# Weight rows laid out as one run per partition, strided columns, a halved last tile and a new order

## Chip, cores and metric

The kernel runs on one core of one Trainium2 chip. The metric is device time of one execution in microseconds: 153.68 us as the median of three runs (153.36 to 154.52). The engines are TensorE (PE, with its weight loads shown apart as PEld), VectorE (DVE), ScalarE (ACT), GpSimd (POOL) and SyncE (SP, which here only issues transfers).

## The reference

Two stages. A gated linear attention runs over 768 steps for 4 x 8 heads of size 48; its output, 3072 tokens of 384, goes through a feed-forward layer whose hidden value is the maximum of three products.

```python
for t in range(S):
    state = alpha[:, :, t, :, None] * state + einsum('bhd,bhe->bhde', k[:, :, t], v[:, :, t])
    y[:, :, t] = einsum('bhd,bhde->bhe', q[:, :, t], state)
x = y.transpose(0, 2, 1, 3).reshape(3072, 384)
h = maximum(maximum(x @ w1, x @ w2), x @ w3)      # w1, w2, w3: 384 x 768
out = h @ w_out                                   # w_out: 768 x 384
```

## The kernel before

The tokens are cut into 12 units (3 stretches of 256 steps for each of 4 batches), each unit into two halves of 4 heads ("pairs" below are numbered 0 to 23) and, for the feed-forward layer, into two tiles of 128 tokens, m = 0 to 23. Each unit needs four loads of 384 KB (alpha, q, k, v; `load`, L262), issued from SP; unit 0 is loaded in halves. The weights are transferred from POOL (`weights`, L272) and turned from f32 to f16 on the way.

The attention of a unit runs through these steps, each with its own engine: the product of the two alphas of a step pair (`aa`, L324, POOL or DVE), its logarithms (L329 and L334, ACT), head totals (L344, PE) and their exponentials (L351), sums of logarithms over the steps (L389, PE; L393, DVE), exponentials of both signs (L398, ACT), scaled q and k (L403, POOL or DVE), their transposes (L421, PE; copied by L429, DVE), scores (L441, PE), masked scores (L449, DVE), the state's sums and carries (L472, L486, L492, L373), and the output y as a sum of two products (L509, L531, PE). Then `xb` copies y from PSUM as f16 times a factor (L247 on ACT, L249 on DVE), L551 transposes it on PE, and L243 copies the transposed tile to `xT`.

The feed-forward layer uses max(a, b, c) = a + max(0, b - a, c - a). `differences` (L281, six instructions on DVE) forms w2 - w1 and w3 - w1 in `wcat`, in place. `bypass` forms w1 @ w_out once: three groups of transposes of `w1s` (L294, PE) and three products (L307), kept in `past`. For each unit, `ffn` has six groups of six matmuls (L575; j = 0 to 2 picks 256 hidden columns, g the difference), with a relu for g = 0 (L584 on ACT, L586 on DVE) and a maximum for g = 1 (L591, DVE), and per tile m one output accumulation of three matmuls with `past` (L603) and six with `wo16` (L606), its copy to `ob` (L243) and its transfer out (L618, SP). The last unit's output accumulations are emitted in two parts, so that the first part needs only two of the three pieces of hT.

No scheduler decides at run time. Every step is registered in a plan; the string `ORDER` lists step numbers with an engine letter and the PSUM banks, and `emit` walks through it. Each engine executes its own instructions in that order and waits where its next instruction isn't ready, so what stands behind a waiting instruction waits too. PSUM has 8 banks, named in `ORDER` as well.

The layouts that the change touches: partition p of `w1s`, `wcat` and `wo16` holds rows p, 128 + p, 256 + p and so on, so one weight row is one contiguous piece of the transfer, and feature tile t of `xT` holds features 128 t to 128 t + 127.

Of the kernel before, what the change touches and what calls it, by code (L numbers as in the profile page):

```python
# [26 lines left out]
6S 0S 3S 1S 2S 52S 5S 7S 8V 9A 4S 10A 11G 17P0 54S 18V 13A 53S 19A 14P1 98S 28P2 12A 20A 55S 29V  # L27
15A 22V 100S 30A 31A 21V 99S 56V 101S 24P3 16G 143S 58A 32V 145S 57A 33V 74P5 144S 59P6 25V 62P7
35P0 146S 23A 63V 205S 26P2 64A 36V 272S 65A 34A 206S 75V 37P0 67G 27V 207S 60A 40P47 77A 274S 76A
61G 339S 66V 208S 42V 78G 69P2 38V 273S 39G 79V 41V 73G 81P5 68A 102G 82V 70V 83P0 80G 104A 44P4  # L30
85G 84V 86P56 45P2 87V 71P0 88V 46A 119P3 72V 103A 47P5 90P2 49A 120V 91P4 122A 193P0 92V 95A 105P1
121A 89V 108P4 93P2 48A 43V 96P3 50P6 123V 51A 94A 124V 109V 126P5 111A 97A 195P7 189V 106A 187V
196A 262P2 127V 321P3 194A 188V 128P5 110A 113V 254P1 112G 129V 258P7 255A 130G 329P0 115P4 192V
330A 197P1 107G 116V 114A 125G 331P6 198A 190V 117P4 325P0 322A 118V 147G 148A 256P1 191V 149A
131P34 263A 257V 153P5 259A 264P2 154V 133V 326A 132V 164P1 260P7 156A 265V 327P0 165V 261V 167A
135P3 323P2 166A 332V 155A 136P7 324V 169G 201P1 140V 158G 150P6 199P5 202A 137A 157V 151A 168V
160P2 328V 171P6 203P1 159A 170G 172V 200A 161V 173P6 204A 175P05 209G 174V 162P2 333P1 211A 163V
276G 277A 210A 218P6 269P7 334A 152G 219V 539S 278A 176V 275S 134V 221A 340S 177V 220A 141P2 229P3
138P1 341S 285P4 222G 230V 179P0 139A 266P6 142V 406S 231A 286V 342S 232A 223V 288A 234G 279P1
180P2 270A 267V 287A 212P3 178V 392P7 181A 233V 213A 296P6 225P4 280A 215G 184A 297V 236P2 290G  # L40
394P1 226V 299A 298A 237V 301G 182P0 393A 388P4 183V 344A 185P5 343G 238P2 395V 224A 227P6 336P0
186A 228V 289G 235A 389A 214G 239V 217G 390P1 337A 216G 345A 292P5 338S 300G 240P74 473S 293V 363P0
352P2 396P3 408S 353V 241V 474S 354A 463P5 391V 397A 268S 242G 398P6 335S 291A 282G 243V 409S 461P7
464A 281G 364V 302G 407S 399V 366A 459P3 284G 271S 365A 244V 476S 245P1 355A 246P5 460V 307P60 671S
357G 247P 462V 605S 294P2 251A 465P4 283G 295V 248A 356G 252P7 411A 455P5 253A 308V 368G 457P1 456A
466V 249P2 359P6 410G 458V 250A 303P3 346P5 529P2 304V 310G 412A 525P1 360V 309G 347A 530A 367G
305P3 311V 369A 361P5 521P7 306V 526A 349G 350G 358A 312P2 523P0 351G 522A 362V 543G 313P1 413P3
419P4 430P7 314P 414A 431V 370P5 420V 433A 467P3 524V 315A 435G 371V 318A 421A 477G 372P0 422A
374P25 545A 470P6 436G 479A 375V 478A 348G 373V 376G 432A 379P4 434G 480P2 471A 403P7 468A 424V
377V 486P0 319P1 423G 404A 531P6 487V 378V 488A 405S 380P3 527P7 481A 532V 608S 320A 541S 489A 381P  # L50
609G 528V 544A 475S 426P1 437P5 382A 540S 415G 316P0 427V 503G 400P7 317A 438V 416G 385V 383P4
552P1 401V 386P2 384A 591P0 483V 387A 402S 553V 484G 428P5 672S 592A 439P3 675G 497P7 555A 655P2
440V 554A 425G 593P0 611A 485G 498V 589P1 500A 418V 429V 491G 546P3 499A 653P4 587P7 417G 654A 594V
441P56 547A 676A 490V 563P4 533P3 442V 588V 443G 444G 656V 661P0 534A 501G 564V 447P5 535S 663P7
590V 662A 606S 492G 677A 446P2 445V 657P3 674S 565A 502G 664V 542S 566A 493P0 448P 658V 472S 482G
556G 504P6 607S 494V 508P4 624A 469S 659P3 452A 449V 610A 618P0 505V 595P1 450P5 453P2 596V 597P6
451A 454A 509V 536P7 660V 511G 549G 619V 568G 598V 621A 506P1 495P4 620A 678P3 551G 537A 725P6 496V
569G 679A 538S 684P0 612P7 719P3 557G 673S 685V 507V 665P4 567G 550V 686A 629P5 695P1 548V 599P2
510V 613A 720A 681V 623V 666A 615V 683V 723P7 622G 696V 630V 698A 602P3 724V 631A 614G 558G 687A
726V 635A 688G 721P4 697A 600V 603A 512P7 700G 601S 513P0 722V 632A 625P1 667S 514P 604S 626V 699G  # L60
574P6 515A 559P3 570P1 518A 727P5 634G 571V 701A 519P7 575V 729P0 616G 728A 560V 577G 516P1 668P2
633G 517V 730V 520V 627P5 669A 572P3 689V 561P0 737P7 670S 617V 573V 731P2 738A 562V 741P7 732A
578P3 576V 745P4 742A 628V 690A 579P0 636P1 580P 637V 640P7 581A 691P5 584V 638P1 746A 582P3 692V
747P0 583A 641V 644P4 743P5 639V 642G 739P6 643G 680V 585P3 645P7 740V 702P1 586A 646P 682V 706P3
703V 647A 734P6 650A 748V 707V 744V 704P1 709G 693P3 759P7 708G 735V 694V 755P0 757P5 705V 711P6
752P3 710P4 761P1 753A 756A 754S 648P2 712P 760A 733S 651P3 649A 749P0 762V 652A 716V 713V 777P7
750A 763P2 751S 736S 717P1 714P3 781P6 718A 779P4 782V 765P0 715V 783P1 778V 799P6 764V 801P3 766V
800A 773P7 784V 775P2 758V 793P0 780V 797P6 774V 795P1 791P5 767P4 792V 802V 770P7 776V 768A 796V
769S 794V 785P5 798V 771V 803P3 786V 772S 787S 807P4 804P 808P 805V 788P2 809A 806S 810S 789A 790S
# [44 lines left out]
def kernel(  # L114
# [82 lines left out]
    xTs = homes(NG, [P, NFT, TG], FP16, "xT")  # L197
# [70 lines left out]
    def weights(g):  # L268
        w, dst = ((moe_w1, moe_w2, moe_w3, moe_w_out)[g],
                  (w1s, wcat[:, :, 0, :], wcat[:, :, 1, :], wo16)[g])  # L270
        plan.step("weights", "POOL", -1.0,
                  lambda eng: nc.gpsimd.dma_start(dst, w.rearrange("(t p) f -> p t f", p=P)),  # L272
                  writes=[("w", g)], size=1.25 if g == 3 else 1.0)


    def differences():
        for g in range(2):
            for j in range(NJ // 2):
                cols = slice(2 * j * P, (2 * j + 2) * P)
                plan.step("d", "DVE", LEAD - 0.5 + 0.5 * g,  # L280
                          lambda eng, g=g, cols=cols: nc.vector.tensor_sub(  # L281
                              wcat[:, :, g, cols], wcat[:, :, g, cols], w1s[:, :, cols]),
                          reads=[("w", 0), ("w", g + 1)], writes=[("d", g, j)])


    def bypass():
        rank = LEAD + 0.5 * SLOPE
        for kt in range(NFT):
            wk = ("wt", kt)

            def turn(eng, kt=kt, wk=wk):
                live[wk] = bank(wk, [P, NJ, P], FP16)
                for j in range(NJ):
                    nc.tensor.transpose(live[wk][:, j, :], w1s[:, kt, j * P:(j + 1) * P], ident)  # L294
# [201 lines left out]
    def output(n):  # L496
# [43 lines left out]
        for i in range(UB):  # L540
# [4 lines left out]
                          eng, xb, live[yk].rearrange("p a b -> p (a b)"), ysc),  # L545
                      reads=[yk], writes=[("xb", m % 3)])

            def turn(eng, xb=xb, xk=xk):
                live[xk] = bank(xk, [P, NFT, P], FP32)
                for ft in range(NFT):  # L550
# [6 lines left out]
                      reads=[xk], writes=[("xT", n, i)])  # L557


    def ffn(n):  # L560
# [32 lines left out]
        for i in range(UB):  # L593
            m = n * UB + i
            r = rank[2 * (NJ // 2) + i]
            ok = ("op", m)
            parts = [(0, NJ)] if n < NG - 1 else [(0, NJ - 2), (NJ - 2, NJ)]
            for lo, hi in parts:
                def shrink(eng, i=i, ok=ok, lo=lo, hi=hi):
                    if lo == 0:  # L600
                        live[ok] = bank(ok, [P, DM], FP32)
                        for kt in range(NFT):
                            nc.tensor.matmul(live[ok], xT[:, kt, i * P:(i + 1) * P],  # L603
                                             past[:, kt, :], start=(kt == 0), stop=False)
                    for kt in range(lo, hi):
                        nc.tensor.matmul(live[ok], hT[:, kt, i * P:(i + 1) * P], wo16[:, kt, :],  # L606
                                         start=False, stop=(kt == NJ - 1))

                plan.step("op", "PE", r + (0.5 if lo else 0.0), shrink,
                          size=hi - lo + (NFT if lo == 0 else 0),  # L610
                          banks=[ok] if lo == 0 else [], writes=[ok],
                          reads=[("hT", n % 3, j) for j in range(lo // 2, hi // 2)]
                          + [("w", 3)]
                          + ([("xT", n, i)] + [("past", kt) for kt in range(NFT)]) * (lo == 0))
            plan.step("ob", "ACT DVE", r, lambda eng, m=m, ok=ok: copy(eng, obs[m % 4], live[ok]),
                      reads=[ok], writes=[("ob", m % 4)])
            plan.step("out", "SP", -2.0,
                      lambda eng, i=i, m=m: nc.sync.dma_start(  # L618
                          out[b * S + (2 * c + i) * P:b * S + (2 * c + i + 1) * P, :], obs[m % 4]),
                      reads=[("ob", m % 4)])  # L620

    load(0, 0, HH, "aqk")
    load(0, HH, H, "a")
    load(0, 0, HH, "v")
    load(0, HH, H, "qkv")
# [49 lines left out]
```

## Time and profile before

| | |
|---|---|
| median of three runs | 153.68 us |
| the profiled execution | 153.0 us |
| its span (first to last instruction) | 151.2 us |
| granted clock | 0.998 |
| PE / DVE / ACT / POOL busy | 133.5 / 120.7 / 82.3 / 69.3 us |
| first matmul of the feed-forward layer (L575) | 28.14 us |
| last matmul ends | 147.85 us |
| issue of w1, w2, w3, w_out on POOL | 15.81, 16.76, 19.09, 30.89 us |

Times inside the execution count from the span's start. An idle engine matters only where the end waits for it. The profile puts a wait down to whatever came last. The chain of work that ended last is followed backwards from the last instruction, and tells which engine or transfer the end hung on at each moment.

### The profile page before, as it was taken

What the parts mean: (1) busy time and instruction counts of PE and PEld (TensorE: products, weight loads), DVE (VectorE), ACT (ScalarE), POOL (GpSimd) and SP (SyncE); (2) the same over time, 40 slices, a digit from 0 to 9 for tenths busy, and PEclk for the clock granted to TensorE, in tenths of its full rate; (3) what the DMA queues carried; (4) which work ended last, traced back from release to release, by engine and by line L of the source; (5) the groups of instructions that cost most, each with busy time, mean ns of one, the idle gap of its engine ahead of it and who ended that gap; (6) DMA issues with size and microseconds to landing.
All of it is one profiled execution on the core that took longest, in us unless ns stands there. A gap on an engine that the chain in (4) does not pass through costs nothing.

```text
span 151.2 us, 5265 instructions
## 1 busy us (share of the span) xinstructions
PE 133.5 (88%) x2220; PEld 102.4 (68%) x2220; DVE 120.7 (80%) x210; ACT 82.3 (54%) x185; POOL 69.3 (46%) x106
## 2 busy tenths in 40 slices
PE   0145498999999999999999999998999999999991
PEld 0133276677766778888677878766868877888660
DVE  3188988769999999999698998899899992395920
ACT  3467246829576996777967756536627305210111
POOL 8114920080390697798992865688800220000000
PEclk9999999999999999999999999999999999999999
DMA  5999999999999999999529929960410002300124
GB/s 127 273 261 261 266 213 211 240 249 221 279 260 262 262 252 261 282 310 270 114 59 259 290 60 259 255 191 0 160 56 0 4 4 81 127 4 0 52 104 156
DMA packets 55880, 26.45 MB, mean 175 GB/s; under 512 B 50737, under 2 KB 55857, under 8 KB 55857
## 3 DMA queue, kind: packets, MB, share of 16 engines
q1 hardware_dynamic: 53440, 23.60, 63.5%
q0 software_dynamic: 1984, 2.36, 9.0%
q8 instruction: 17, 0.28, 0.8%
q10 hardware_dynamic: 432, 0.17, 0.5%
q14 instruction: 7, 0.05, 0.1%
HBM read 23.76 MB, written 4.72 MB: 188 GB/s over the span
## 4 chain that ended last, share of the span: by engine, by line
PE 74%; DMA 11%; SPq 5%; DVE 3%; issue 3%; ACT 2%; POOL 1%; ACTq 0%; DVEq 0%; POOLq 0%
PE psum L575 31%; PE psum L606 14%; PE psum L603 7%; DMA wcat<-in_moe_w_dram 7%; SPq L262 5%; PE psum L441 4%; DMA qn<-in_q_dram 4%; PE psum L421 4%; PE psum L531 3%; PE psum L472 3%; PE psum L551 2%; PE psum L307 2%; PE psum L509 2%; PE psum L389 1%; DVE Z L373 1%
## 5 line engine op out<-in xcount | busy, mean ns | idle before, releaser
L575 PE MATMUL psum<-xT,wcat 128*128 128x256 f16 x432 | 55.3, 277 | 0.3 <-DVE wcat L281 0.3
L575 PEld LDWEIGHTS <-wcat 128*128 128x128 f16 x432 | 40.7, 99 | 6.6 <-DVE wcat L281 0.5
L449 DVE TENSOR_TENSOR LA<-psum,d 128x1024 f16<-128x1024 f32 x24 | 28.8, 1219 | 3.8 <-PE psum L441 2.6
L606 PE MATMUL psum<-wo,hT 128*128 128x384 f16 x144 | 27.3, 326 | 0.0
L591 DVE TENSOR_TENSOR hT<-psum,hT 128x512 f16<-128x512 f32 x36 | 23.8, 681 | 3.2 <-PE psum L531 2.8
L403 POOL TENSOR_TENSOR qk<-qn,ep 128x384 f16<-128x384 f32 x16 | 16.7, 1052 | 14.5 <-ACT ep L398 14.0
L243 ACT COPY ob<-psum 128x384 f32<-128x384 f32 x17 | 8.1, 484 | 24.7 <-PE psum L606 24.7
L403 POOL TENSOR_TENSOR qk<-kn,en 128x384 f16<-128x384 f32 x15 | 15.0, 1001 | 13.0 <-ACT en L398 8.5
L606 PEld LDWEIGHTS <-hT 128*128 128x128 f16 x144 | 14.1, 98 | 9.3
L584 ACT ACTIVATE hT<-psum 128x512 f16<-128x512 f32 x25 | 14.6, 600 | 8.1 <-PE psum L575 7.9
L429 DVE COPY qkT<-psum 128x1024 f16<-128x1024 f16 x24 | 16.0, 684 | 1.4 <-PE psum L421 1.1
L603 PE MATMUL psum<-past,xT 128*128 128x384 f16 x72 | 15.7, 327 | 0.0
L421 PE MATMUL psum<-d,qk 64*128 64x64 f16 x384 | 10.6, 200 | 5.2 <-DVE qk L403 4.0
L398 ACT ACTIVATE en<-psum 128x384 f32<-128x384 f32 x24 | 11.8, 496 | 5.3 <-DVE psum L393 4.1
L398 ACT ACTIVATE ep<-psum 128x384 f32<-128x384 f32 x24 | 11.7, 492 | 4.6 <-POOL qk L403 2.9
L373 POOL TENSOR_TENSOR Z<-U,G 48x192 f16<-48x192 f32 x12 | 6.0, 504 | 16.3 <-DVE U L486 15.8
L421 PEld LDWEIGHTS <-qk 64*128 64x128 f16 x384 | 8.1, 100 | 8.0 <-DVE qk L403 5.3
L243 ACT CAST xT<-psum 128x384 f16<-128x384 f32 x19 | 8.8, 483 | 6.0 <-PE psum L551 5.7
L324 POOL TENSOR_TENSOR aa<-an 128x384 f32<-128x384 f32 (+1 forms) x11 | 10.7, 972 | 2.6 <-DMA an<-in_alpha_dram 2.5
L247 ACT ACTIVATE xb<-psum,c 128x384 f16<-128x384 f32 x17 | 9.4, 580 | 4.2 <-PE psum L531 4.1
L586 DVE TENSOR_SCALAR hT<-psum 128x512 f16<-128x512 f32 x11 | 7.5, 686 | 4.4 <-PE psum L575 4.3
L247 ACT ACTIVATE v<-vn,c 128x384 f16<-128x384 f32 x14 | 8.6, 617 | 4.3 <-DMA vn<-in_v_dram 3.9
(54 smaller groups left out, 193.8 us busy)
## 6 DMA issues: line engine op xcount, KB each, us to landing
out_dram<-ob SPq DMA_DIRECT2D x24, 192.0 KB, 2.0
an<-in_alpha_dram SPq DMA_DIRECT2D x11, 384.0 KB, 6.1
kn<-in_k_dram SPq DMA_DIRECT2D x11, 384.0 KB, 5.9
qn<-in_q_dram SPq DMA_DIRECT2D x11, 384.0 KB, 6.5
vn<-in_v_dram SPq DMA_DIRECT2D x11, 384.0 KB, 6.1
wcat<-in_moe_w_dram POOLq DMA_DIRECT2D x2, 576.0 KB, 11.3
w1s<-in_moe_w_dram POOLq DMA_DIRECT2D x1, 576.0 KB, 8.0
wo<-in_moe_w_out_dram POOLq DMA_DIRECT2D x1, 576.0 KB, 7.6
```

What stands on the lines that cost most here:

```text
L243: (nc.scalar.copy if eng == "ACT" else nc.vector.tensor_copy)(out=out, in_=in_)
L247: nc.scalar.activation(out=out, in_=in_, func=AFT.Copy, scale=factor)
L398: lambda eng, t=t, sign=sign: nc.scalar.activation(out=t, in_=live[Lk], func=AFT.Exp, scale=sign),
L403: lambda eng, w=w, x=x, e=e: on[eng].tensor_mul(qk[:, w, :, :, :D].rearrange("p r h d -> p h r d"), ld[x][n % NL][:, hs], e),
L421: nc.tensor.transpose(live[tk][:, i, at:at + HALF], qk[rows, w, r, 2 * j:2 * j + 2, :], ident[rows, rows])
L429: lambda eng: nc.vector.tensor_copy(out=qkT.rearrange("p i w j t -> p i (w j t)"), in_=live[tk]),
L449: lambda eng: nc.vector.tensor_mul(LA.rearrange("p a j r t -> p (a j) (r t)"), live[Ak].rearrange("p a (j t) -> p (a j) t", j=2), maskA.un ...
L575: nc.tensor.matmul(live[gk][:, jj, :], wcat[:, kt, g, c0:c0 + P], xT[:, kt, :], start=(kt == 0), stop=(kt == NFT - 1))
L584: nc.scalar.activation(out=h, in_=live[gk], func=AFT.Relu)
L591: lambda eng, h=h, gk=gk: nc.vector.tensor_max(h, live[gk], h),
L603: nc.tensor.matmul(live[ok], xT[:, kt, i * P:(i + 1) * P], past[:, kt, :], start=(kt == 0), stop=False)
L606: nc.tensor.matmul(live[ok], hT[:, kt, i * P:(i + 1) * P], wo16[:, kt, :], start=False, stop=(kt == NJ - 1))
```

## The change

It has four parts.

The weight transfers read rows 3p to 3p + 2 (for w_out rows 6p to 6p + 5) to partition p, one run of memory for each partition. Feature tile t therefore holds features 3p + t, and hidden tile j the hidden columns 6c + j. To match, `xb` is written permuted (feature 3f + t to place 128 t + f), and the differences and the transposes of w1 read every sixth column.

w2 and w3 arrive in tiles of their own, `raw`, from which the differences are written to `wcat`. `raw` shares its memory with the `xT` of units 6 to 11, whose copies therefore wait for all differences.

The last tile, m = 23, is computed, copied and sent out in two halves of 192 columns.

`ORDER` is replaced as a whole (815 steps in place of 811): other positions, other choices of engine, other banks. For the start of the kernel: ahead of the first weight POOL has a scaled k and a scaled q product (before, likewise two, in between others); the order of issue there is w1, `aa` of unit 2, w2, w3, three scaled products, w_out (before: w1, w2, `aa`, a copy of v, w3, a scaled product, w_out). SP issues alpha of unit 1 first, and then q, k, v of unit 1, alpha, k, q of unit 2, alpha of unit 3, v of unit 2 (before: k, q of unit 1, alpha of unit 2, v of unit 1, k, q, v of unit 2, alpha of unit 3). DVE takes 13 of the 48 scaled products (before 17) and 3 of the 32 carries that can go to either engine (before 9).

```diff
-    xTs = homes(NG, [P, NFT, TG], FP16, "xT")
+    early = homes(NG // 2, [P, NFT, TG], FP16, "xT")
+    late = homes(2, [P, 3, NFT, TG], FP16, "xU")
+    xTs = early + [late[i // 3][:, i % 3] for i in range(NG - NG // 2)]
+    raw = [t.rearrange("p a b c -> p (a b c)").rearrange("p (k f) -> p k f", k=NFT) for t in late]
...
         w, dst = ((moe_w1, moe_w2, moe_w3, moe_w_out)[g],
-                  (w1s, wcat[:, :, 0, :], wcat[:, :, 1, :], wo16)[g])
+                  (w1s, raw[0], raw[1], wo16)[g])
+        t = NJ if g == 3 else NFT
         plan.step("weights", "POOL", -1.0,
-                  lambda eng: nc.gpsimd.dma_start(dst, w.rearrange("(t p) f -> p t f", p=P)),
+                  lambda eng: nc.gpsimd.dma_start(
+                      dst.rearrange("p t f -> p (t f)"),
+                      w.rearrange("(p t) f -> p (t f)", t=t)),
...
+    def columns(w, j, n):
+        return w.rearrange("p k (c j) -> p k j c", j=NJ)[:, :, j:j + n, :]
...
                           lambda eng, g=g, j=j, cols=cols: nc.vector.tensor_sub(
-                              wcat[:, :, g, cols], wcat[:, :, g, cols], w1s[:, :, cols]),
+                              wcat[:, :, g, cols].rearrange("p k (j c) -> p k j c", j=2),
+                              columns(raw[g], 2 * j, 2), columns(w1s, 2 * j, 2)),
...
-                    nc.tensor.transpose(live[wk][:, j, :], w1s[:, kt, j * P:(j + 1) * P], ident)
+                    nc.tensor.transpose(live[wk][:, j, :], columns(w1s, j, 1)[:, kt, 0, :],
+                                        ident)
...
                       lambda eng, xb=xb, yk=yk: scaled(
-                          eng, xb, live[yk].rearrange("p a b -> p (a b)"), ysc),
+                          eng, xb.rearrange("p (t f) -> p f t", t=NFT),
+                          live[yk].rearrange("p a b -> p (a b)").rearrange(
+                              "p (f t) -> p f t", t=NFT), ysc),
...
-                      reads=[xk], writes=[("xT", n, i)])
+                      reads=[xk] + [("d", g, j) for g in range(2) for j in range(NJ // 2)] * (n >= NG // 2),
+                      writes=[("xT", n, i)])
...
+            wide = 1 if m < NG * UB - 1 else 2
+            for half in range(wide):
+                cols = slice(half * DM // wide, (half + 1) * DM // wide)
+                ok = ("op", m, 1)[:2 + half]
+                home = (m + half) % 4
...
+                                live[ok] = bank(ok, [P, cols.stop - cols.start], FP32)
...
+                                                 past[:, kt, cols], start=(kt == 0), stop=False)
...
+                          lambda eng, home=home, rows=rows, cols=cols: nc.sync.dma_start(
+                              out[rows, cols], obs[home][:, cols]),
```

More of the change, by code (lines that the diff above doesn't have):

```diff
@@ L26 @@
 ORDER = """
[L27 to L67, printed above, removed]
@@ L68 @@
-800A 773P7 784V 775P2 758V 793P0 780V 797P6 774V 795P1 791P5 767P4 792V 802V 770P7 776V 768A 796V
-769S 794V 785P5 798V 771V 803P3 786V 772S 787S 807P4 804P 808P 805V 788P2 809A 806S 810S 789A 790S
+52S 0S 3S 1S 2S 6S 5S 56V 57A 4S 7S 8G 53S 10A 11G 9A 17P0 54S 58A 18V 13A 55S 62P1 12A 28P2 20A
+14P3 98S 74P4 29V 15A 63V 100S 19A 22V 30A 99S 21V 31A 143S 16V 24P5 33V 101S 32V 59P7 144S 23G 25V
+35P2 60A 145S 34A 75V 26P5 146S 64A 36V 77A 205S 27V 37P2 65A 40P07 272S 76A 206S 78V 207S 42V 79G
+41V 208S 38V 44P1 66G 339S 68A 81P4 273S 80A 67V 45P6 274S 61V 39G 82V 103A 275S 69P2 70V 83P4 102G
@@ new lines @@
+84V 86P02 73G 104A 406S 46A 119P3 87V 85G 108P4 49A 120V 71P5 109V 122A 88V 121A 72V 124G 90P1 111A
+110A 47P0 123V 91P3 43V 112G 126P4 95A 89V 197P6 113G 92V 407S 50P7 193P1 127V 198A 341S 93P2 130G
+51V 48A 128P3 96P5 94A 115P6 97A 195P0 194A 187V 196A 188V 254P2 105P5 116V 321P1 189V 258P0 322A
+325P6 129V 329P7 192V 117P3 330A 262P1 191V 255A 264P7 259A 190V 263A 327P2 106A 118V 331P0 326A
+107G 147G 148A 256P1 265V 114G 323P5 149A 328V 125A 164P6 260P3 324V 131P47 165V 153P2 199P5 132V
+166A 133V 167A 168G 154V 135P4 261V 155A 201P6 200A 169G 257V 156A 150P3 136P5 332V 151A 158G 171P1
@@ new lines @@
+202V 203P3 140A 172V 137A 157G 134V 141P0 173P4 204A 209G 142V 160P1 210A 138P6 161V 333P7 159G
+211A 174V 139A 170G 152G 218P3 276G 212P0 229P1 175P26 219V 213A 230V 162P4 220A 177V 392P0 221A
+163V 231A 269P3 393A 233G 176V 278A 277A 223G 285P4 179P5 334A 279P0 286V 266P2 270A 178V 335S 222G
+232A 342S 288A 234V 280A 225P6 271S 287A 180P3 282V 235A 215G 340S 226V 236P0 216G 388P4 181A 473S
+184V 283G 539S 237V 394P6 343G 389A 296P7 185P3 267A 238P0 224G 297V 186A 227P4 268S 395V 182P2
+217G 344A 336P3 408S 228V 214G 183A 290G 345A 298A 289G 239V 352P6 299A 363P2 396P4 337A 240P57
@@ new lines @@
+284G 338S 397A 353V 292P0 300G 364V 390P3 474S 355A 241V 411A 409S 293V 245P4 242G 365A 463P5 605S
+243G 354A 391V 459P0 302A 301G 464V 366A 398P1 291A 410V 246P6 294P2 460A 244V 368G 247P 412A 295V
+307P50 248A 455P7 251A 281V 249P4 308V 346P2 456A 419P3 457P6 420V 310G 347A 399V 252P5 349G 461P7
+309G 253A 458V 357G 250A 430P2 465P1 311V 421A 529P5 422A 462V 356G 369A 521P6 466V 358G 303P3 431V
+359P0 351G 530V 674S 432A 467P7 367G 433A 542S 360V 522A 606S 304V 348G 477G 361P0 475S 468V 305P5
@@ new lines @@
+413P2 476S 313P3 306V 350G 525P4 414A 671S 523P7 526A 362V 312P2 478A 374P56 314P 375V 370P0 470P4
+318A 524V 376G 315A 377G 371V 479A 416G 435G 544A 378V 319P5 316P3 471A 486P7 372P0 380P2 434V
+379P6 403P4 373V 543G 415G 545A 609G 487V 381P 317A 404V 489A 437P0 480P3 385V 405S 320A 400P4 382A
+438V 469S 481A 417V 488A 482G 425A 424G 386P2 497P5 439P0 387A 498V 383P6 440V 436A 552P3 423G
+546P7 527P2 547A 610A 587P7 418G 384A 553V 401V 531P0 558G 588A 491G 402S 589P1 611A 532V 541S 499A
+653P6 483G 528V 492A 540S 484G 657P4 554A 490V 607S 661P7 569G 654V 608S 658A 591P0 675G 555A 590V
@@ new lines @@
+472S 662A 426P2 672S 592V 441P64 563P1 612P7 442V 595P0 613A 500A 427V 443G 663P6 501G 428P2 664V
+593P7 444G 564V 533P5 485G 429V 565A 557G 677A 676A 594V 446P6 503A 502G 447P2 655P3 445V 534A 566A
+448P 615G 548G 656V 596A 567G 504P4 508P7 452A 449V 493P0 556G 684P3 505V 453P2 597P6 454A 509V
+549G 618P4 659P5 568G 685V 619V 450P2 598V 536P7 620A 510G 451A 494V 511G 687A 551G 660V 621A 629P6
+678P2 622G 723P0 537A 630V 679A 538S 686A 495P4 550G 506P1 535S 727P7 496V 673S 719P3 728A 507V
+513P4 631A 665P5 720A 633G 632A 724A 681G 512P7 623G 695P1 570P2 666A 696V 514P 571V 559P5 635G
@@ new lines @@
+698A 574P0 515V 599P2 697A 690G 575V 518A 689G 560V 572P0 688V 600A 561P3 699V 516P7 601S 729P5
+562V 634G 517A 725P6 617G 578P2 730V 519P7 577G 602P3 520A 726V 683G 624A 616G 573V 576G 745P4 603A
+682G 579P5 604S 691P6 701G 746A 640P3 692V 614G 636P0 680G 580P 700V 625P6 721P4 584A 581V 637V
+585P5 668P2 586V 722V 747P0 626V 669A 582P1 670S 638P4 583A 627P6 737P2 639V 731P1 738A 641V 643V
+642V 741P4 628V 645P5 763P2 742A 748V 732A 644P3 702P6 733S 646P 703V 706P4 650A 759P1 707V 647V
+693P6 708G 704P4 739P0 709G 694V 743P3 705V 734P6 740V 711P7 760V 710P4 761P5 764V 712P 744V 648P0
@@ L70 @@
+765P1 735V 716A 651P2 752P3 736S 652V 667S 649V 713V 755P6 714P7 773P2 715V 717P0 753V 777P4 718V
+757P7 778V 779P3 762V 791P0 780V 781P4 756V 775P5 758V 795P3 782V 783P6 774V 749P7 766V 784V 799P4
+792V 796A 797P2 750A 800A 751S 770P1 798V 754S 776V 793P6 767P3 794V 771V 801P0 768V 785P7 769S
+772S 788P4 786V 802V 787S 807P2 789A 803P5 790S 808P 804P 809A 811P6 810S 805V 812P 806S 813A 814S
 """
@@ L280, in differences @@
                 plan.step("d", "DVE", LEAD - 0.5 + 0.5 * g,
-                          lambda eng, g=g, cols=cols: nc.vector.tensor_sub(
-                              wcat[:, :, g, cols], wcat[:, :, g, cols], w1s[:, :, cols]),
+                          lambda eng, g=g, j=j, cols=cols: nc.vector.tensor_sub(
+                              wcat[:, :, g, cols].rearrange("p k (j c) -> p k j c", j=2),
+                              columns(raw[g], 2 * j, 2), columns(w1s, 2 * j, 2)),
                           reads=[("w", 0), ("w", g + 1)], writes=[("d", g, j)])
@@ L595, in ffn @@
             r = rank[2 * (NJ // 2) + i]
-            ok = ("op", m)
+            rows = slice(b * S + (2 * c + i) * P, b * S + (2 * c + i + 1) * P)
             parts = [(0, NJ)] if n < NG - 1 else [(0, NJ - 2), (NJ - 2, NJ)]
[L598 to L620, printed above, removed]
+            wide = 1 if m < NG * UB - 1 else 2
[3 more added lines that the diff above has]
+                home = (m + half) % 4
+                for lo, hi in parts:
+                    def shrink(eng, i=i, ok=ok, lo=lo, hi=hi, cols=cols):
+                        if lo == 0:
+                            live[ok] = bank(ok, [P, cols.stop - cols.start], FP32)
+                            for kt in range(NFT):
+                                nc.tensor.matmul(live[ok], xT[:, kt, i * P:(i + 1) * P],
+                                                 past[:, kt, cols], start=(kt == 0), stop=False)
+                        for kt in range(lo, hi):
+                            nc.tensor.matmul(live[ok], hT[:, kt, i * P:(i + 1) * P],
+                                             wo16[:, kt, cols], start=False,
+                                             stop=(kt == NJ - 1))
+                    plan.step("op", "PE", r + (0.5 if lo else 0.0), shrink,
+                              size=(hi - lo + (NFT if lo == 0 else 0)) / wide,
+                              banks=[ok] if lo == 0 else [], writes=[ok],
+                              reads=[("hT", n % 3, j) for j in range(lo // 2, hi // 2)]
+                              + [("w", 3)]
+                              + ([("xT", n, i)]
+                                 + [("past", kt) for kt in range(NFT)]) * (lo == 0))
+                plan.step("ob", "ACT DVE", r,
+                          lambda eng, ok=ok, home=home, cols=cols: copy(
+                              eng, obs[home][:, cols], live[ok]),
+                          reads=[ok], writes=[("ob", home)], size=1 / wide)
+                plan.step("out", "SP", -2.0,
+                          lambda eng, home=home, rows=rows, cols=cols: nc.sync.dma_start(
+                              out[rows, cols], obs[home][:, cols]),
+                          reads=[("ob", home)], size=1 / wide)
```

## The prediction, made before the changed kernel ran

> **What bounds the kernel now.** I read the head of the profile first, then a table of stretches, then the chain of work that ended last, then single rows. Head and slices (tenths of each fortieth of the span):
>
> ```profile
> PE 133.5 (88%) x2220; PEld 102.4 (68%) x2220; DVE 120.7 (80%) x210; ACT 82.3 (54%) x185; POOL 69.3 (46%) x106
> ...
> PE   0145498999999999999999999998999999999991
> ...
> DVE  3188988769999999999698998899899992395920
> ...
> DMA  5999999999999999999529929960410002300124
> ```
>
> TensorE is idle in the first seven slices and the last, and nowhere else to speak of. In the table of stretches (us, then busy time and instructions of PE, weight load, DVE, ACT, POOL, then clock, DMA share, GB/s):
>
> ```profile
> 15.00:20.00 5.00, 2.67 (x60) 1.89 (x62) 4.52 (x8) 1.14 (x2) 4.88 (x6) 1.00 1.26 256
> 20.00:25.00 5.00, 4.59 (x115) 3.97 (x112) 3.84 (x7) 2.91 (x7) 0.00 (x0) 1.00 1.15 209
> 25.00:30.00 5.00, 4.38 (x40) 3.10 (x39) 4.23 (x10) 4.11 (x10) 0.12 (x1) 1.00 1.15 229
> 30.00:40.00 10.00, 10.00 (x141) 7.84 (x138) 8.31 (x14) 5.93 (x12) 3.50 (x5) 1.00 1.18 249
> ...
> 145.00:151.20 6.20, 2.83 (x18) 1.48 (x16) 0.56 (x1) 0.96 (x2) 0.00 (x0) 0.96 0.34 122
> ```
>
> From 30 us on PE is full. The chain (start, length, what) shows what it waits for before that, and the end:
>
> ```profile
> 8.27 6.08 DMA qn<-in_q_dram
> 14.49 1.37 POOL qk L403
> 15.93 0.84 issue
> 16.76 10.67 DMA wcat<-in_moe_w_dram
> 27.53 0.57 DVE wcat L281
> 28.14 2.74 PE psum L575 x12
> ...
> 146.86 0.99 PE psum L606 x6
> 147.91 0.48 ACT ob L243
> ```
>
> So: loads, a POOL product, the weight transfer behind it, one difference on DVE, and from 28.14 us the first feed-forward matmul (L575). From there to the last matmul's end at 147.85 are 119.7 us, with 0.53 us idle in the stretches after 30. The time is therefore (start of L575) + (PE work that is still to do then) + (stalls) + (tail from the last matmul to the span's end, 151.2 - 147.85 = 3.35 us). Only these four can move. The sums are made against this execution, 153.0 us with a span of 151.2; the median of the three runs is 153.68, 0.68 more, and I add that at the end.
>
> **Part 1, contiguous weight rows.** The two DMA rows:
>
> ```profile
> q1 hardware_dynamic: 53440, 23.60, 63.5%
> q0 software_dynamic: 1984, 2.36, 9.0%
> ```
>
> In the packet records of the trace q0 (the weights) has 1152 packets of 1536 B at 134.7 ns and 768 of 768 B at 80.5 ns, q1 (loads) packets of 384 B at about 35 ns beside them. A line through the two q0 sizes gives 26 ns + 70.6 ns per KB (1000 B), so one 4608 B packet takes 352 ns (estimate), and a weight takes 8 per engine in place of 24. While weights move, the records show one q1 packet for each q0 packet, and the slowest engine needs 3.56 us per weight: 24 x (134.7 + 35) = 4.07 nominal, a factor of 0.875. After: 8 x (352 + 35) = 3.10 nominal, 2.7 with the factor. Two weights must land before the first difference: 5.4 to 6.2 us in place of 7.1. If a run of 4608 B still moves as three packets, nothing is gained; that end stays in the range.
>
> The start: the first weight is issued at 15.81 after POOL's q product (14.49 to 15.86). In the new order POOL does two products ahead of it, the first on k of unit 1, which is now the seventh whole load, as q was, so at 14.45; with 1.0 us each (row of L403 on POOL: 1001 ns) the issue comes at 16.5, 0.7 later. That is partly covered: in the records the slowest engine still moves the q load of unit 2 until 20.6, which is the same eleventh load. From 20.6 the second weight lands at 26.0 to 26.8 (27.43 before). The second issue now also stands behind aa of unit 2 (its load is ninth, 17.3 us; 1.0 us on POOL), so at 18.4, ahead of its turn on the engines.
>
> [...]
>
> **Part 2, differences on strided operands.** Six instructions on DVE (L281) now read every sixth element. Before:
>
> ```profile
> 27.53 1.03 DVE L281 TENSOR_TENSOR wcat<-wcat,w1s 128x768 f16<-128x768 f16 x2 [0.77 <-DMA wcat<-in_moe_w_dram]
> ```
>
> 0.55 us for 768 elements, while the f32 rows of DVE lie on one element per ns: 384 in 0.55, 512 in 0.68, 1024 in 1.22 (L403, L591, L449). On that line 768 take 0.95. No row has a stride of 12 B, so the bounds are 0.55 (nothing lost) and 1.75 (two cycles an element). I take 0.95, the row's line: 2.4 us more in all, 0.4 on the path ahead of the first matmul.
>
> **Part 3, the order ahead of L575.** Counted on PE: before, the first L575 stands behind 6 L389, 3 L344, 5 L421 groups, 4 L441, 2 L472, 2 L509, 2 L531, 4 L551 and 2 L294; after, behind one L421 group, one L441 and one L294 more and one L344 fewer. By the chain's lengths (0.36, 0.35, 0.44, 0.19) that is 0.96 us of PE work moved to where PE is idle. It must not delay the first L575: between its first product on q of unit 1 (14.0 to 14.5) and the first difference DVE has 3 L449 (1.23), 3 L429 (0.68), 3 L403 (0.55), 4 L373 (0.35), 2 L393 (0.35), 2 adds (0.53), a G (0.3), an xb (0.6) and an xT (0.55), 12.0 us, so it gets there at 26.0 to 26.5, about with the weight; with 0.95 the difference is there at 27.0 to 27.75. On PE, the L441 of pair 5 waits for its copy (DVE, 25.4 to 26.0), and behind it stand 1.3 to 2.0 us: 26.7 to 28.0. I take 27.9 for the first L575, near the upper ends because these walks leave out the handover between engines: 0.24 earlier.
>
> Then PE takes six g = 0 groups (0.66 each) before the first that needs the third weight. With 0.95 per difference from 26.8 on, DVE ends them at 27.75, 28.7, 30.3, 32.5, 33.5, 34.4 (the copy and masked product of pairs 4 and 5 between), and PE wants them at 27.9, 29.4, 30.7, 32.4, 33.15, 34.8: stalls of about 0.1 + 0.35, less what lies idle already, 0.3.
>
> **Part 4, the rest.** The strided weight transposes (18 x L294, 0.44 per six) lie in PE's idle time; at twice that they cost 1.3 us, half of it covered. xb is written with a stride of 256 B: no such row; 24 x 0.58, off the path, from nothing to 24 x 0.58 more on ACT and DVE; nothing taken, since ACT is 54% busy. The new wait (late xT on all differences) is over 30 us early. On the remaining order: PE had no stall to win, so I give it nothing.
>
> **Part 5, the last tile in halves.** 9 matmuls of 384 (0.163 each) become 18 of 192; L551 moves 128 columns in 0.057 with its load, so 192 in 0.082: no more, at most 0.3 (if the 98 ns of a weight load showed). The last copy falls from 0.48 to 0.36 (row of 192, L334 on ACT), and 96 KB leave in place of 192, taken as 0.1: -0.2, against +0.05.
>
> Sum: -0.24 - 0.96 + 0.3 - 0.2 + 0.05 = -1.05. Execution 151.95, median 153.68 - 1.05 = 152.6.
>
> **Rivals.** (a) Slower: the strided reads. If a difference takes 1.75, the last of the six ends 4.8 us later, at 39.2, while PE wants it at 34.8 and has only in-order work behind: 4.4 of stall for 0.3, and 0.8 on the first. Time 152.6 + 4.1 + 0.8 = 157.5; at 1.35, half of that, 155.0. It decides from about 1.15 us a difference, where the 1.05 is gone. Against it: no DVE row shows less than one element per ns. [...]
> (b) No change: packets do not grow or gain, the second weight lands at 27.7 + 0.7 of later issue = 28.1 (the backlog not covering), L575 starts at 29.05, +0.9 in place of -0.24: 153.7.
> (c) Larger gain: weights at 26.0, differences stay at 0.55, L575 at 26.9 and no stall: -1.24 - 0.96 - 0.2 = -2.4: 151.3. POOL idle for 9.98 us before 29.88 speaks for it, DVE's 12.0 us of queue against.
>
> **How the numbers follow.** A measurement here can tell about 1%, 1.54 us, from no change. Forecast 0.50 (own range 151.8 to 153.3, two fifths of it beyond 1%), (c) 0.17, (b) 0.17, (a) 0.16. Faster by over 1%: 0.20 + 0.17 = 0.37; within: 0.30 + 0.17 = 0.47; slower: 0.16. The range goes from below (c) to the 1.35 us case of (a): 151.0 to 155.0.
>
> **What would show it.** q0 with some 576 packets and a smaller share; the second weight landed by 26.8; L281 near 0.95; L575 starting near 27.9; about 118.75 us from there to the last matmul; a tail near 3.15. Wrong if PE shows idle time between 28 and 40 that waits for L281 or for alpha of unit 3, or if gaps open later, where I assume none.

## The result, and the profile after

The changed kernel takes 169.65 us (median of four runs, 168.85 to 172.14) against 153.52 us for the kernel before beside it: a ratio of 1.102 with a 95% interval of 1.095 to 1.110. The prediction was 152.6 us with a range of 151.0 to 155.0. The profiled execution took 169.51 us, its span is 167.7.

The head of the page and the same slices as before:

```profile
PE 138.5 (83%) x2229; PEld 103.8 (62%) x2229; DVE 133.2 (79%) x205; ACT 100.6 (60%) x179; POOL 75.0 (45%) x118
...
PE   0267548999879899499878999699898989799993
...
DVE  3399669999857999478949989977988999897621
ACT  3664498566879999854889849768454341203011
```

TensorE, full from the eighth slice on before, now has a hole every few slices to the end of the kernel. ACT has 18.3 us more work and DVE 12.5 us more. The costliest groups tell whose (count, then busy time and mean ns of one, then the idle time before it and what ended it):

```profile
L250 ACT ACTIVATE xb<-psum,c 128x384 f16<-128x384 f32 x16 | 31.0, 2063 | 8.6 <-PE psum L566 5.4 <-PE psum L544 3.1
...
L252 DVE TENSOR_SCALAR xb<-psum,c 128x384 f16<-128x384 f32 x8 | 15.8, 1979 | 0.1
L566 PE MATMUL psum<-d,xb 128*128 128x128 f16 x72 | 9.0, 240 | 7.7 <-ACT xb L250 5.8 <-DVE xb L252 1.8
...
L292 DVE TENSOR_TENSOR wcat<-xU,w1s 128x768 f16<-128x768 f16 x6 | 6.9, 1205 | 0.0
```

The rows of xb and of the transpose behind it (L551, now L566) in the kernel before:

```profile
L247 ACT ACTIVATE xb<-psum,c 128x384 f16<-128x384 f32 x17 | 9.4, 580 | 4.2 <-PE psum L531 4.1
L551 PE MATMUL psum<-d,xb 128*128 128x128 f16 x72 | 7.8, 235 | 0.0
...
L249 DVE TENSOR_SCALAR xb<-psum,c 128x384 f16<-128x384 f32 x7 | 4.2, 608 | 0.7 <-ACT en L398 0.7
```

One xb took 580 ns on ACT and 608 on DVE before; it now takes 2063 and 1979, with the same element count. PE waits 7.7 us directly for it at L566, where it waited for nothing before. The chain shows the rest; this is a stretch of it in the middle of the kernel:

```profile
80.67 0.42 PE psum L544 x32
...
81.30 1.34 issue
82.64 2.23 ACT xb L250
84.91 0.34 PE psum L566 x3
...
88.37 2.16 DVE xb L252
90.53 0.52 DVE qkT L442
91.05 0.95 DVE Z L386
...
92.27 1.14 DVE LA L462
93.45 4.09 PE psum L591 x36
```

The output product L544 ends, two xb follow each other on ACT (the 1.34 us put down as "issue" lie inside the first, which runs from 81.17 to 83.14), and only as each is done can its L566 go, and what is queued behind it on PE. Five microseconds later an xb on DVE holds up a copy, a carry and a masked product that have nothing to do with it but stand behind it. That is how an operation which is no bound by its sum becomes one: 14.4% of the span, 24 us, is xb on the chain, where it was not in the prediction's chain at all.

The six differences (L292) take 1.2 us each in place of 0.55 (0.68 on average), and the first feed-forward matmul (L591) starts at 31.10 us in place of 28.14. More than half of that delay is xb's as well: with xb written contiguously the start is at 29.50 (the first run below). On the chain ahead of it stand three xb and no difference:

```profile
20.08 3.67 ACT xb L250 x2
...
26.42 1.94 DVE xb L252
```

The second weight had landed at 26.91; DVE came to the first difference only at 29.24, behind that xb and two copies, and had it done at 30.42, while PE was at the products ahead of L591 until 31.0.

### The profile page after: what moved, and what is told of

Its sections match the earlier page's. It is cut to its first block, busy times and chain, and to the rows that moved or that the text cites. A ratio compares the mean times of both kernels' runs of the same rounds, so it can differ in the third digit from the quotient of the medians.

```text
span 167.7 us, 5275 instructions
## 1 busy us (share of the span) xinstructions
PE 138.5 (83%) x2229; PEld 103.8 (62%) x2229; DVE 133.2 (79%) x205; ACT 100.6 (60%) x179; POOL 75.0 (45%) x118
## 4 chain that ended last, share of the span: by engine, by line
PE 60%; ACT 12%; DVE 11%; DMA 7%; issue 4%; SPq 4%; POOL 1%; ACTq 0%; DVEq 0%; POOLq 0%
PE psum L591 27%; PE psum L627 11%; ACT xb L250 10%; DMA an<-in_alpha_dram 7%; PE psum L624 6%; DVE xb L252 5%; SPq L265 4%; PE psum L454 3%; PE psum L566 3%; PE psum L434 2%; PE psum L544 2%; PE psum L522 2%; PE psum L485 2%; DVE qkT L442 2%; DVE LA L462 1%
## 5 line engine op out<-in xcount | busy, mean ns | idle before, releaser
L591 PEld LDWEIGHTS <-wcat 128*128 128x128 f16 x432 | 41.4, 100 | 8.4 <-issue 1.7
L250 ACT ACTIVATE xb<-psum,c 128x384 f16<-128x384 f32 x16 | 31.0, 2063 | 8.6 <-PE psum L566 5.4
L462 DVE TENSOR_TENSOR LA<-psum,d 128x1024 f16<-128x1024 f32 x24 | 29.1, 1227 | 4.9 <-PE psum L454 4.8
L591 PE MATMUL psum<-xT,wcat 128*128 128x256 f16 x216 | 29.0, 287 | 1.3 <-ACT xb L250 1.2
L627 PE MATMUL psum<-wo,hT 128*128 128x384 f16 (+1 forms) x150 | 27.5, 320 | 0.0
L591 PE MATMUL psum<-xU,wcat 128*128 128x256 f16 x216 | 27.4, 273 | 0.0
L627 PEld LDWEIGHTS <-hT 128*128 128x128 f16 x150 | 14.5, 98 | 8.9
L252 DVE TENSOR_SCALAR xb<-psum,c 128x384 f16<-128x384 f32 x8 | 15.8, 1979 | 0.1
L566 PE MATMUL psum<-d,xb 128*128 128x128 f16 x72 | 9.0, 240 | 7.7 <-ACT xb L250 5.8
L246 ACT COPY ob<-psum 128x384 f32<-128x384 f32 (+1 forms) x16 | 7.6, 479 | 12.2 <-PE psum L627 12.2
L454 PE MATMUL psum<-qkT 48*64 48x128 f16 x384 | 11.0, 239 | 4.4 <-ACT xb L250 2.9
L406 DVE TENSOR_TENSOR psum<-psum,la 128x192 f32<-128x192 f32 x24 | 8.2, 360 | 7.1 <-PE psum L402 6.3
L402 PE MATMUL psum<-la,c 128*128 128x192 f16 x24 | 6.0, 272 | 8.5 <-ACT la L347 8.5
L434 PE MATMUL psum<-d,qk 64*128 64x64 f16 x384 | 11.1, 202 | 1.9 <-DVE qk L416 1.9
```

What stands on the lines that cost most here:

```text
L250: nc.scalar.activation(out=out, in_=in_, func=AFT.Copy, scale=factor)
L252: on[eng].tensor_scalar(out=out, in0=in_, scalar1=factor, scalar2=1.0, op0=AOP.mult, op1=AOP.mult)
L434: nc.tensor.transpose(live[tk][:, i, at:at + HALF], qk[rows, w, r, 2 * j:2 * j + 2, :], ident[rows, rows])
L454: nc.tensor.matmul(live[Ak][i * HALF:(i + 1) * HALF, p, at:at + P], qkT[rows, i, 1, j, r * HALF:(r + 1) * HALF], qkT[rows, i, 0, j, :], st ...
L462: lambda eng: nc.vector.tensor_mul(LA.rearrange("p a j r t -> p (a j) (r t)"), live[Ak].rearrange("p a (j t) -> p (a j) t", j=2), maskA.un ...
L591: nc.tensor.matmul(live[gk][:, jj, :], wcat[:, kt, g, c0:c0 + P], xT[:, kt, :], start=(kt == 0), stop=(kt == NFT - 1))
```

## Experiments

The question was which of three things costs the time: the strided write of xb, the strided differences, or the new order.

**The strided write undone.** xb is written contiguously, and the transpose behind it picks the features by its weight load, with a step of 6 bytes.

```diff
-                          eng, xb.rearrange("p (t f) -> p f t", t=NFT),
-                          live[yk].rearrange("p a b -> p (a b)").rearrange(
-                              "p (f t) -> p f t", t=NFT), ysc),
+                          eng, xb, live[yk].rearrange("p a b -> p (a b)"), ysc),
...
-                    nc.tensor.matmul(live[xk][:, ft, :], xb[:, ft * P:(ft + 1) * P], order,
+                    nc.tensor.matmul(live[xk][:, ft, :],
+                                     xb.rearrange("p (f t) -> p t f", t=NFT)[:, ft, :], order,
```

> The changed kernel with one thing undone: xb is written contiguously again (0.58 to 0.61 us before, 2.06 on ACT and 1.98 on DVE after), and the permutation is read by the weight load of the following transpose (L566), with a step of 6 bytes. Theory X (the strided write of xb is the whole loss): xb back at 0.6, the gaps of PE that end on xb gone, and the time at 151 to 154 us, where the prediction was. Theory O (the new order stalls by itself): xb back at 0.6 but the time stays above 160. Theory D (the strided differences, 1.2 us each, delay the first feed-forward matmul by 3 us and that is kept to the end): 156 to 158. If strided weight loads are slow instead, PEld of L566 goes from 0.10 to 0.2 or more each, 72 of them, and PE gets up to 7 us longer.

Measured: 151.91 us, ratio 0.994 (0.991 to 0.997) to the kernel before. The groups of xb and of the weight load that now does the permutation (L564 is the former L566):

```profile
L250 ACT ACTIVATE xb<-psum,c 128x384 f16<-128x384 f32 x16 | 8.8, 578 | 9.7 <-PE psum L564 5.8 <-PE psum L544 3.9
L564 PE MATMUL psum<-d,xb 128*128 128x128 f16 x72 | 8.6, 236 | 0.0
...
L564 PEld LDWEIGHTS <-xb 128*128 128x128 f16 x72 | 6.0, 110 | 1.1 <-issue 0.2
```

xb is back at 578 ns, PE no longer waits for it, and a weight load costs 110 ns against 106 without the step. This one write was the whole loss, and more: 17.7 us by the two medians.

**The permutation on the other side of the same instruction**: write contiguously, read PSUM with a step of 12 bytes.

```diff
-                          eng, xb.rearrange("p (t f) -> p f t", t=NFT),
+                          eng, xb.rearrange("p (t f) -> p t f", t=NFT),
...
-                              "p (f t) -> p f t", t=NFT), ysc),
+                              "p (f t) -> p t f", t=NFT), ysc),
```

> The changed kernel with the permutation of xb moved to the other side of the same instruction: it writes contiguously and reads PSUM with a step of 12 bytes. Theory W (only the step of the write costs): xb at about 0.6, the time as in the run with the plain xb. Theory S (any long step costs, whichever side): xb at about 2 us, the time at 168 to 171. Between the two, an xb of 1.0 to 1.2 us would give 156 to 162.

151.84 us, ratio 0.993 (0.990 to 0.996); xb at 578 ns on ACT and 609 on DVE. Only the write's step costs.

**The order alone**: all old layouts, with the new order, the halved tile and the separate tiles for w2 and w3.

```diff
-                  lambda eng: nc.gpsimd.dma_start(
-                      dst.rearrange("p t f -> p (t f)"),
-                      w.rearrange("(p t) f -> p (t f)", t=t)),
+                  lambda eng: nc.gpsimd.dma_start(dst, w.rearrange("(t p) f -> p t f", p=P)),
...
-        return w.rearrange("p k (c j) -> p k j c", j=NJ)[:, :, j:j + n, :]
+        return w.rearrange("p k (j c) -> p k j c", j=NJ)[:, :, j:j + n, :]
```

(and xb written contiguously, with the old transpose behind it)

> The new order, the halved last tile and the separate tiles for w2 and w3, but all the old layouts (rows t*128+p, contiguous columns, plain xb): the order by itself. Theory X: 152 to 154, and the differences at 0.55 again. Theory O: above 160, with PE gaps at the same places as in the changed kernel. Weights by 1536-byte packets take 3.56 us each on the slowest engine again.

150.85 us, ratio 0.985 (0.982 to 0.988). The order does not stall; with the halved tile it is worth 1.5%, more than was expected of it here, and more than the 0.96 + 0.15 us (0.7%) that the prediction gave the two.

**The strided write in the kernel before**, in its own order, with w1 to w3 in rows 3p + t so that the features match.

```diff
-                  lambda eng: nc.gpsimd.dma_start(dst, w.rearrange("(t p) f -> p t f", p=P)),
+                  lambda eng: nc.gpsimd.dma_start(
+                      dst, w.rearrange("(p t) f -> p t f", t=NFT) if g < 3
+                      else w.rearrange("(t p) f -> p t f", p=P)),
...
-                          eng, xb, live[yk].rearrange("p a b -> p (a b)"), ysc),
+                          eng, xb.rearrange("p (t f) -> p f t", t=NFT),
+                          live[yk].rearrange("p a b -> p (a b)").rearrange(
+                              "p (f t) -> p f t", t=NFT), ysc),
```

> The kernel before, in its own order, with w1, w2 and w3 in rows 3p+t (three pieces per partition in wcat) and xb written with the step of 256 bytes: the strided write by itself, everything else as before. Theory X: xb at 2.0 us and the time at 165 to 172. Theory O (the loss is of the new order): within 3 us of 153.5. An xb that is slow but hidden would leave 154 to 157.

174.22 us, ratio 1.139 (1.134 to 1.145), xb at 2040 and 1961 ns. The loss belongs to the write, in either order; it is somewhat larger than expected.

**What one xb costs by its step**: each xb of the plain run with a step of its own.

```diff
+        if eng == "DVE" and k == 0:
+            nc.vector.tensor_scalar(out=wr(xb, 192), in0=rd(y, 192), scalar1=factor, scalar2=1.0, op0=AOP.mult, op1=AOP.mult)
...
+        if eng == "ACT" and k == 9:
+            nc.scalar.activation(out=rows(xb, 3), in_=rds(y, 3), func=AFT.Copy, scale=factor)
```

> What one xb costs by the step of its innermost dimension: in the run with the plain xb each of the eight xb on DVE writes with another step (4, 8, 16, 32, 64, 128, 256, 384 bytes), the first eight on ACT likewise, the last eight on ACT write contiguously and read PSUM with steps of 8 to 384 bytes. The features of x are thereby permuted per tile, so the result isn't the layer's. If the cost comes with any step beyond one element, all writes take 2 us; if it comes with leaving a line of some size, there is a step at one place, and 256 bytes lies at the top with 2.0 (1.98 on DVE, 2.06 on ACT). Reads of PSUM stay near 0.58 up to 12 bytes by the run with the permuted read; unknown beyond.

The features are mixed in this run, so its own time (164.05 us, one execution) says nothing of the layer; only the rows count, each one instruction. On DVE the write steps are 4 bytes (L274), 8 (L276), 16 (L278); on ACT 4 (L290), 8 (L292), 16 (L294); L320 reads PSUM with 384 bytes:

```profile
L294 ACT ACTIVATE xb<-psum,c 128x384 f16<-128x384 f32 x1 | 2.0, 1991 | 0.9 <-PE psum L610 0.9
...
L278 DVE TENSOR_SCALAR xb<-psum,c 128x384 f16<-128x384 f32 x1 | 1.9, 1937 | 0.1
...
L292 ACT ACTIVATE xb<-psum,c 128x384 f16<-128x384 f32 x1 | 1.1, 1095 | 0.0
L276 DVE TENSOR_SCALAR xb<-psum,c 128x384 f16<-128x384 f32 x1 | 1.1, 1083 | 0.0
L290 ACT ACTIVATE xb<-psum,c 128x384 f16<-128x384 f32 x1 | 0.7, 674 | 0.0
L274 DVE TENSOR_SCALAR xb<-psum,c 128x384 f16<-128x384 f32 x1 | 0.6, 647 | 0.0
...
L320 ACT ACTIVATE xb<-psum,c 128x384 f16<-128x384 f32 x1 | 0.6, 581 | 6.8 <-PE psum L630 6.8
```

Against the 578 and 609 ns of a contiguous write, a step of 4 bytes costs 1.1 to 1.2 times as much, 8 bytes 1.8 to 1.9 times, and 16 bytes 3.2 times on DVE and 3.4 on ACT. There it stays up to 384 bytes (1852 to 2217 ns). An estimate from these rows: 0.2 us and 384 elements at 4.6 ns each give 1.97 us, as from 16 bytes on; at half of 4.6 ns an element it is 1.08 us, as at 8 bytes, and at a quarter 0.64 us, as at 4. What lies behind these prices the runs don't show. Both engines show them alike. ACT reads PSUM at no extra cost at any step from 8 to 384 bytes (573 to 605 ns), and DVE at 12 bytes (609 ns, the run with the permuted read).

**The columns contiguous**: plain xb, and unit steps in the differences and the transposes of w1 (w_out by its old rows). Of the new layouts only the one run per partition of w1 to w3 stays.

```diff
-        return w.rearrange("p k (c j) -> p k j c", j=NJ)[:, :, j:j + n, :]
+        return w.rearrange("p k (j c) -> p k j c", j=NJ)[:, :, j:j + n, :]
```

> The run with the plain xb, and besides the columns contiguous again (differences and transposes of w1 read unit steps, w_out by its old rows): of the new layouts only the one run per partition of w1, w2 and w3 is left. Theory D2 (the strided differences, 1.2 in place of 0.55 us, are what the plain-xb run loses against the order alone): differences at 0.55 and 150.6 to 151.1, with the order alone at 150.85. If the packets of 4608 bytes bring something of their own, as the prediction had it, the second weight lands 0.5 to 1 us earlier than in the order-alone run and the time is 149.8 to 150.4. If it stays at 151.9, the loss is not of the differences.

150.03 us, ratio 0.985 (0.979 to 0.992), differences at 0.55. The plain-xb run's 0.994 against 0.985 suggests a price of about 1% for the strided columns; the two intervals still touch, and w_out's rows changed with the columns. The pair of runs with the fill below settles both. The second weight landed at 27.7, 0.7 earlier than with the old rows, and the time lies in the range expected if the long packets brought something. But the ratio is that of the order alone, so no gain of theirs is shown.

**The second weight issued earlier**, in the order alone and in the contiguous-column run: on POOL, w2 and w3 directly behind w1.

```diff
-41V 208S 38V 44P1 66G 339S 68A 81P4 273S 80A 67V 45P6 274S 61V 39G 82V 103A 275S 69P2 70V 83P4 102G
-84V 86P02 73G 104A 406S 46A 119P3 87V 85G 108P4 49A 120V 71P5 109V 122A 88V 121A 72V 124G 90P1 111A
+41V 208S 38V 44P1 66G 339S 68A 81P4 273S 80A 67V 45P6 274S 61V 39G 73G 85G 82V 103A 275S 69P2 70V 83P4 102G
+84V 86P02 104A 406S 46A 119P3 87V 108P4 49A 120V 71P5 109V 122A 88V 121A 72V 124G 90P1 111A
```

(39G is w1, 102G `aa` of unit 2, 73G w2, 85G w3)

> The order alone (old layouts), with one move on POOL: the issues of w2 and w3 come directly behind w1, ahead of the product of alphas of unit 2, which waits for its load until 18.6. Theory I (the second weight is bound by its issue at 19.6, not by its transfer): issued near 17, landed 2.9 to 3.6 us behind the first, at 27.2 to 27.9 in place of 28.5, the first feed-forward matmul 0.6 to 1.3 us earlier and the time 149.5 to 150.3. Rival (the transfer or DVE's queue binds anyway): 150.6 to 151.1. If the alphas get late by it, above 151.

> The contiguous-column run with the same move on POOL: long packets where the transfer and not the issue sets the second weight. If 8 packets of 4608 bytes per engine take 2.7 to 3.1 us against 2.9 to 3.6 for 24 of 1536, the second weight lands up to 0.6 us earlier than in the run with old rows and the same move, and the time is 0 to 0.6 us below it. If the packets bring nothing, the two are equal within 0.3 us.

150.42 us (0.987, 0.981 to 0.993) and 150.39 us (0.987, 0.982 to 0.993): neither better than without the move, and equal to each other, so the long packets save no time here either. First the trace with old rows, then that with long runs:

```profile
27.66 1.03 DVE L290 TENSOR_TENSOR wcat<-xU,w1s 128x768 f16<-128x768 f16 x2 [0.94 <-DMA xU<-in_moe_w_dram]
...
28.89 0.82 PE L587 MATMUL psum<-xT,wcat 128*128 128x256 f16 x6
```

```profile
27.08 1.03 DVE L293 TENSOR_TENSOR wcat<-xU,w1s 128x768 f16<-128x768 f16 x2 [0.27 <-DMA xU<-in_moe_w_dram]
...
28.83 0.82 PE L591 MATMUL psum<-xT,wcat 128*128 128x256 f16 x6
```

The first difference begins 0.9 and 1.5 us earlier than the 28.54 of the order alone, as the weight is there earlier, but PE is not: it begins the first feed-forward matmul at 28.9 and 28.8, 0.7 us and 1.2 us after that difference is done, because its own transposes and score products ahead of it are not done. The bound has changed hands.

**PE kept busy.** Why is PE late? Its small matmuls at 20 to 28 us take about 1.5 times what the same shapes take later (six transposes of w1 0.82 us there, 0.50 when PE runs at full rate). In the kernel before, the first twelve feed-forward matmuls do too:

```profile
28.14 2.74 PE L575 MATMUL psum<-xT,wcat 128*128 128x256 f16 x12 [0.28 <-DVE wcat L281]
30.81 0.62 PE L441 MATMUL psum<-qkT 48*64 48x128 f16 x16
```

2.74 us for 12, where 6 take 0.65 later. The granted clock in the profile stays at 1.00 through these stretches (the table in the prediction, 20 to 30 us), so it does not show it. Three runs ask whether the work that PE has done before sets the moment of the faster rate: they put small matmuls on constants into banks that the next step overwrites, where PE waits.

```diff
+    def idle_fill(key, n):
+        for _ in range(n):
+            nc.tensor.matmul(psall[:, place[key], :P], tri, ident, start=True, stop=True)
```

> The contiguous-column run with 22 small matmuls (128 columns, constants, into banks that the next step overwrites) put on PE where it waits between 18.7 and 23.9 us; the result is the same. In the earlier traces a matmul of 256 columns takes 0.22 us until some moment and 0.11 from then on: 30.75 us in the kernel before, about 27.3 in this run without the fill, 33.3 with the strided differences. [...] Rival (the rate is not PE's own history): the fill only delays, 150 to 151.5.

> The kernel before with 14 such matmuls where PE waits between 20 and 26.5 us. [...] Rival: 153 to 154.

> The run with the plain xb (strided differences, 1.2 us each) with the same 22 matmuls. If its 1.0 to 1.9 us against the contiguous-column run come from DVE (differences later), they stay: 150.2 to 151.0 with the fill, 1.0 or more above the filled contiguous run. If they come from PE staying at half rate longer, they go: within 0.4 us of it.

The kernel before with 14 of them takes 152.33 us, ratio 0.996 (0.993 to 0.999): more work and, by a gain close to the noise, less time. The trace is clearer:

```profile
28.43 1.49 PE L584 MATMUL psum<-xT,wcat 128*128 128x256 f16 x12 [0.95 <-DVE wcat L286]
29.84 0.42 PE L449 MATMUL psum<-qkT 48*64 48x128 f16 x16
```

The twelve now take 1.49 us in place of 2.74, and the sixteen score products 0.42 in place of 0.62. So the faster rate came earlier with more work in PE's waits; how much work it takes these runs don't show.

In the contiguous-column run the fill brought full rate at 24.8 us, but the time stayed at 150.25 us (0.982, 0.978 to 0.987), above the 148.8 to 149.5 that the author had expected of the earlier full rate: there PE then waits 1.01 us for the differences. In the plain-xb run with strided differences it gave 151.93 us (0.993, 0.990 to 0.995). So these two runs, measured side by side, stay 1.7 us apart with PE at full rate in both from before the first feed-forward matmul. The chain of the second shows where; this is the stretch behind its second difference:

```profile
30.23 0.60 DVE qkT L449
30.83 1.11 DVE wcat L297
31.93 1.13 DVE LA L469
33.07 2.25 DVE wcat L297 x2
35.36 2.79 PE psum L599 x24
```

DVE is full with the differences and what stands between them, and PE waits for it. The last six feed-forward matmuls ahead of the first product with w_out start at 38.14 us, against 36.55 with unit steps: 1.6 of the 1.7 us are lost by then. The cost of the strided columns is therefore DVE's, not PE's, and the rows of w_out have no part in it.

**Both remedies**: early issue, contiguous columns and the fill.

> The contiguous-column run with both remedies for its head: w2 and w3 issued directly behind w1, and the 22 small matmuls that fill PE's waits. With the early issue alone the weight was there at 27.08 but PE reached the first feed-forward matmul only at 28.8, at half rate; with the fill alone PE was there at 27.7 and waited for the weight until 28.7. If the two bounds are all there is, both together give a first matmul at 27.5 to 27.9 and 149.0 to 149.7 us. Rival (a third bound stands right behind, DVE's or POOL's queue): 150.0 to 150.6, no better than either alone.

149.81 us, ratio 0.978 (0.974 to 0.982), just above the expected range; the first feed-forward matmul starts at 27.56, inside it. It is the fastest version that ran, though its interval overlaps that of the fill alone: the start is 1.1 us earlier than there, but the stretch to the last matmul is 0.7 us longer (117.6 against 116.9), and why was not traced.

## Why the prediction was wrong

The step that failed is in Part 4: "xb is written with a stride of 256 B: no such row; 24 x 0.58, off the path, from nothing to 24 x 0.58 more on ACT and DVE; nothing taken, since ACT is 54% busy." Both halves were wrong. The size: 16 x 1.48 + 8 x 1.37 = 34.7 us more by the two rows' means, against an upper bound of 13.9. And the path: a busy share of 54% does not mean that a wait of 1.4 us is covered, since xb stands between L531 and L551 in every unit, with two xb in a row on one engine and in-order engines behind. The runs showed both: 24 us of xb on the chain, the time back at 151.91 us without the strided write, and 174.22 us with it in the old order. In the stretch of the changed kernel shown above, PE still has products of L434, L624 and L627 to do until 82.87 us, and then waits 0.33 us before the first L566 and 1.37 us before the second, each for its xb.

The rival that ended slower named the right kind of cause, a long step in SBUF, at the wrong instruction: it priced the reads of the differences and left the write of xb out. Its 1.75 us a difference was the author's estimate, the f32 rows' line with the slope doubled; no run shows it, the differences took 1.2. What a long step costs a write no row showed beforehand. Measured, steps of 8 and 16 bytes (4 and 8 elements of f16) make it cost 1.8 and more than 3 times as much: 1083 and 1937 ns on DVE against 609, 1095 and 1991 on ACT against 578.

Point by point, with the write undone (that run's ratio of 0.994 is what 152.8 would be beside the 153.68 of the prediction, and 152.6 was forecast), the terms were right only in their sum. The trace of that run is of its slowest execution, 153.03 us.

- Long packets: right. 576 packets in q0; 4608 B took 360 ns (352 estimated), and with early issue the second weight came 3.0 us after the first against 3.56 with 1536 B, by the packet records. Yet they saved no time, as the runs above show.
- The second weight at 26.0 to 26.8: 26.91 in the changed kernel itself, 28.1 in the plain-xb run, 27.7 in the run with the permuted read. The step "at 18.4, ahead of its turn on the engines" failed: `aa` waited for its load until 18.6 and the issue came at 19.6. In all three traces hardly a packet of a weight starts between 22 and 23 us, and those of the second begin at 23.2 to 23.4; with the early issue they follow the first weight's without a gap. Why the landing differs by up to 1.2 us among the three was not traced.
- Differences at 0.95: mis-sized, 1.2. That is past the 1.15 at which rival (a) was to decide. By Part 2 and the rival's prices, 1.2 in place of 0.55 would cost 0.7 + 1.5 = 2.2 us; the runs show 1.1 (plain xb against the order alone) to 1.7 (the two runs with the fill).
- L575 at 27.9: 29.5 in the plain-xb run and 29.1 in that with the permuted read, by these two.
- The order given nothing, since "PE had no stall to win": wrong. In the order-alone run PE needs 116.86 us from the first feed-forward matmul to the last matmul (29.15 to 146.01), against 119.7. Of the 2.85 us, 0.96 is the work moved ahead, as counted, and 1.4 the half-rate start of the twelve matmuls (2.74 us in place of twice 0.65), which the stretches count as busy and which the order-alone run doesn't have. The remaining 0.5 was not traced to one place.
- The tail: 3.15 forecast, 2.89 in the order-alone run; the last copy takes 0.32.
- One slip that changes nothing above: of the range 151.8 to 153.3 about a quarter, not two fifths, lies more than 1% below 153.68.

That the forecast of the plain-xb run came out near is therefore no support for its terms.

## What to carry to other kernels

When a permutation has to go somewhere, price every operand whose innermost step becomes long, the write first: here the same permutation costs 34.7 us of engine time and 17.7 us of the kernel's as a write to SBUF, nothing as a read of PSUM, and some 5 ns for each of 72 loads as a weight load. An operation without a row in the trace needs its bound from the hand-over it sits in and from its engine's order, not from the engine's busy share. And a "busy" PE in the first stretches can be one at half rate, as here (0.22 us a matmul of 256 columns in place of 0.11): compare the length of the same shape early and late before calling a stretch full.

## What the runs showed of the hardware that was not expected

Writes of f16 to SBUF by ACT and DVE, from f32 in PSUM: 0.58 to 0.61 us for 384 elements with unit step, 0.65 to 0.67 at 4 bytes, 1.08 to 1.10 at 8, 1.85 to 2.22 from 16 to 384 bytes. Matmuls of 256 columns, in the kernel before: every 0.22 us in the first stretch (12 in 2.74, from 28.14 us) and every 0.11 later (6 in 0.65), with the granted clock shown as 1.00 in both. With 14 useless matmuls in the waits the first twelve took 1.49 us, and that kernel was faster by 0.4% (0.1 to 0.7%).
